# Attention and a gated MLP on one core: four engines pinned to source order, a pair's scores issued in two runs, query block 8 first

## The chip, the cores and the metric

The kernel runs on one core of a Trainium2 chip. The metric is device microseconds of one execution (lower is better); before the change the median of three runs is 756.76 us (756.08 to 757.27).

A core has four compute engines here: TensorE (PE, with PEld for its weight loads), VectorE (DVE), ScalarE (ACT) and GpSimd (POOL). SyncE (SP) issues most DMAs. PE writes its results into PSUM banks, from which DVE and ACT read them.

## What is computed

```python
def _attn_ref(q, k, v):                       # 8 batches, 8 heads, 576 x 64
    scores = scale * np.matmul(q, k.transpose(0, 1, 3, 2))
    mask = block_i >= block_j                 # causal in blocks of 64
    scores = np.where(mask, scores, -1000000000.0)
    scores = scores - np.max(scores, axis=-1, keepdims=True)
    attn = np.exp(scores)
    attn = attn / (np.sum(attn, axis=-1, keepdims=True) + 1e-09)
    return np.matmul(attn, v)

def _moe_ref(x, w_in, w_spatial, b_spatial, w_out):
    h = np.maximum(x @ w_in, 0.0)             # 576 x 512 -> 576 x 1024
    u, v = (h[..., :d_ff // 2], h[..., d_ff // 2:])
    v_n = (v - mu) / np.sqrt(var + 1e-06)     # mu, var over the 512 columns
    v_s = np.einsum('ts,bsd->btd', w_spatial, v_n) + b_spatial[None, :, None]
    return (u * v_s) @ w_out

# reference: x is the attention's output, heads side by side; result = _moe_ref(x, ...)
```

All values are float32.

## The kernel before

**Tiling.** The work of the attention is 32 pairs of heads (8 batches, 4 pairs). The 576 queries are cut into four blocks of 128 (0 to 3) and one of 64 (called block 8 in the change's title; index 4 in `SLOTS`). A pair has seven slots, `(head, first block, last block)`: head 0 and head 1 for blocks 0-1, for block 2, for block 3, and one slot (head 2 in the code's count) that holds the last 64 queries of both heads. Batches 1 to 7 split q and k into a high and a low float32r part (`prep_pair`: two casts "hi" on ACT, four subtractions "lo" on POOL) and compute three products per score tile; batch 0 uses the raw float32 values.

**Steps.** The main loop runs over steps; a pair has seven (`NS`), so step n belongs to pair g = n // 7 with i = n % 7. In each step the code issues, in this order:

- loads and the start of `prep_pair` for the next pair (DMAs on SP);
- `due(0)`: what earlier steps put off with `later`, for example evacuations on ACT and gates on DVE;
- scores on PE: `scores` (L270) for slots 0-1 at i = 0, 2-3 at i = 1, 4-5 at i = 2, and `scores_last` (L290) for the 64-query slot at i = 5 (in batch 0 four slots at i = 0). A score matmul of `scores` contracts 64 rows, one head's half of the partitions (L285); one of `scores_last` contracts 128 rows (L297). The banks come from `s_bank` (L266), a pool of four, and in batch 0 partly from the second pool of four;
- `av` (L453), the output products of an earlier pair: 16 steps after that pair's start (`AV_AT`), or 9 in batch 0 and for the very last pair (`BOOT_AV`). `x_evac` (L431) then casts the result on ACT and subtracts on DVE, one step later in batches 1 to 7, at once in batch 0;
- `exps` (L304) of slot i: scale, mask and row maximum on DVE (L320, L329), exponential with row sum on ACT (L336);
- `transposes` of finished slots on DVE (L406, L411), by the table `TURNS`, and after the last slot `move` (L415): sixteen DMAs on SP (L421) that bring the transposed tile into the one buffer `turned`, from which `av` reads. Batch 0 and the last pair transpose on PE instead (`transposes_pe`, L383) and copy on ACT (L384);
- `norm` (L341): two small operations on DVE (L347, L350), multiplications on POOL (L354);
- `due(1)`, then background work: conversion of the weights (`prep_w`, `prep_w_sp`, `split`) and `prep_pair`;
- groups of the MLP (`moe`) on PE, about one a step, when a batch's attention is done: `v_group` (L515), `u_group` (L609), `sp_group` (L633, gate L642, split L651 and L652), `out_group` (L668, L676);
- `due(2)` and `due(3)`.

Where `b_sp`, the weights and the initial tiles are prepared, the code is as it stands in the listing below.

**What sets the order.** The kernel is traced in this order, but the framework's scheduler decides in which order each engine's instructions are issued: it ranks them by a model of its own, and an instruction whose inputs it takes as ready early may go ahead of others that stand before it in the source. Semaphores follow from the tiles' accesses. Each engine then runs its queue in that fixed order.

Buffers that matter: scores have four PSUM banks (tag "s"), everything else four (tag "m"); "hi" and "lo" two each; the raw q and k one; the probabilities "p" five; the transposed tiles "q" two; `turned` one.

Of the kernel before, what the change touches and what calls it, by code (L numbers as in the profile page):

```python
# [28 lines left out]
SLOTS = [(0, 0, 1), (1, 0, 1), (0, 2, 2), (1, 2, 2), (0, 3, 3), (1, 3, 3), (2, 4, 4)]  # L29
# [4 lines left out]
LAST, AV_AT, BOOT_AV = 5, 2 * NS + 2, NS + 2  # L34
# [7 lines left out]
def kernel(  # L42
# [35 lines left out]


# [7 lines left out]
    for _ in range(6):  # L87
        nc.tensor.matmul(warm[:, :P], mask[:, :P], mask[:, :P], start=True, stop=True)
# [31 lines left out]
    def split(hi, lo, raw):  # L120
        nc.scalar.copy(hi, raw)
        yield
        nc.gpsimd.tensor_tensor(out=lo, in0=raw, in1=hi.bitcast(F32), op=ALU.subtract)
        yield

    def prep_w(hi, lo, w, rows, cols, name):
# [55 lines left out]
    def prep_w_tail():  # L182
# [6 lines left out]
        nc.scalar.copy(ws_a, r[:, :S])  # L189
        nc.scalar.copy(ws_b[64:65, :], r[64:65, S:2 * S])  # L190
        yield
        nc.gpsimd.tensor_tensor(
            out=ws_b[0:64, :], in0=r[0:64, :S], in1=ws_a[0:64, :].bitcast(F32), op=ALU.subtract
        )
        nc.scalar.copy(ws_b[96:97, :], r[96:97, S:2 * S])
        yield
        nc.gpsimd.tensor_tensor(
            out=ws_b[96:97, :], in0=r[96:97, S:2 * S], in1=ws_b[96:97, :].bitcast(F32),
            op=ALU.subtract,
        )  # L200
# [31 lines left out]
    def prep_pair(b, pr):  # L232
# [33 lines left out]
    def s_bank(b, nm, other):  # L266

        if b == 0 and other:
            return ps_m.tile([P, 512], F32, tag="m", name=f"s_{nm}")
        return ps_s.tile([P, 512], F32, tag="s", name=f"s_{nm}")  # L270

    def scores(b, pr, slots):

        parts = operands(b, pr)
        for i in slots:
            banks[(b, pr, i)] = s_bank(b, f"{b}_{pr}_{i}", slots[0] == 4)
        for i in slots[::2]:
            o = 0
            for t in range(SLOTS[i][1], SLOTS[i][2] + 1):
                n = P * (t + 1)  # L280
                qs = slice(S + t * P, S + (t + 1) * P)
                for m, (a, k) in enumerate(parts):
                    for hd in range(2):
                        js = slice(64 * hd, 64 * hd + 64)
                        nc.tensor.matmul(  # L285
                            banks[(b, pr, i + hd)][:, o:o + n], a[js, qs], k[js, :n],
                            start=(m == 0), stop=(m == len(parts) - 1),
                        )
                o += n

    def scores_last(b, pr):
        parts = operands(b, pr)
        bk = [s_bank(b, f"{b}_{pr}_{NS - 1}_{z}", False) for z in range(2)]
        banks[(b, pr, NS - 1)] = bk
        for z in range(2):
            for m, (a, k) in enumerate(parts):
                nc.tensor.matmul(  # L297
                    bk[z][:, :HT], a[:, Q8:], k[:, z * HT:(z + 1) * HT],
                    start=(m == 0), stop=(m == len(parts) - 1),
                )  # L300
# [3 lines left out]
    def exps(b, pr, i):  # L304
# [10 lines left out]
        if hd < 2:  # L315
            o = 0
            runs = []
            for r, t in enumerate(range(t0, t1 + 1)):
                n = P * (t + 1)
                nc.vector.tensor_tensor_reduce(  # L320
                    out=pt[:, o:o + n], in0=bk[:, o:o + n], in1=mask[:, 512 - n:], scale=-0.125,
                    scalar=BIG, op0=ALU.add, op1=ALU.min, accum_out=nmax[:, r:r + 1],
                )
                runs.append((o, n, nmax[:, r:r + 1]))
                o += n
        else:
            for z in range(2):
                zs = slice(z * HT, (z + 1) * HT)
                nc.vector.tensor_tensor_reduce(  # L329
# [3 lines left out]
                )  # L333
            runs = [(0, S, nmax[:, 1:2])]
        for r, (o, n, mx) in enumerate(runs):
            nc.scalar.activation(  # L336
                pt[:, o:o + n], pt[:, o:o + n], AF.Exp, bias=mx, scale=-1.0,
                accum_out=ssum[:, s0 + r:s0 + r + 1],
            )
        ptiles[(b, pr, i)] = (pt, ssum, runs)  # L340

    def norm(b, pr, i):

        both = [ptiles[(b, pr, j)] for j in ((i - 1, i) if i < NS - 1 else (i,))]
        ssum = both[0][1]
        n = sum(len(runs) for _, _, runs in both)
        nc.vector.tensor_scalar(  # L347
            out=ssum[:, 0:n], in0=ssum[:, 0:n], scalar1=EPS_SM, scalar2=None, op0=ALU.add
        )
        nc.vector.reciprocal(ssum[:, 4:4 + n], ssum[:, 0:n])  # L350
        r = 4
        for pt, _, runs in both:
            for o, w, mx in runs:
                nc.gpsimd.tensor_scalar(  # L354
                    out=pt[:, o:o + w], in0=pt[:, o:o + w], scalar1=ssum[:, r:r + 1],
                    scalar2=1.0, op0=ALU.mult, op1=ALU.mult,
                )
# [8 lines left out]
    def transposes_pe(b, pr, i):  # L366
# [15 lines left out]
        for c in range(n):  # L382
            nc.tensor.transpose(bk[:, c * P:(c + 1) * P], pt[:, c * P:(c + 1) * P], ident)  # L383
        nc.scalar.copy(  # L384
            to[:, :, o:o + 32 * n].rearrange("p a (c j) -> p c a j", j=32),
            bk[:, :n * P].rearrange("p (c a j) -> p c a j", a=4, j=32),
        )
        if hd == 2:
            bk = bank(f"{i}c4")
            nc.tensor.transpose(bk[0:64, 0:P], pt[:, 4 * P:S], ident)  # L390
            nc.scalar.copy(
                to[0:64, :, Q8O + P:], bk[0:64, 0:P].rearrange("p (a j) -> p a j", j=32)
            )

    def transposes(b, pr, i):
# [10 lines left out]
        nc.vector.transpose(  # L406
            to[:, :, o:o + 32 * n].rearrange("p r (c j) -> p c r j", j=32),
            pt[:, :n * P].rearrange("p (c r j) -> p c r j", r=4, j=32),
        )
# [23 lines left out]
    def x_evac(b, pr, av, q0, n):  # L433
        qs = slice(q0, q0 + n)

        def hi():
            x = x_tiles(b, pr)
            nc.scalar.copy(x[:, 0, qs], av[:, :n])

        def lo():  # L440
            x = x_tiles(b, pr)
            nc.vector.tensor_tensor(  # L442
                out=x[:, 1, qs], in0=av[:, :n], in1=x[:, 0, qs].bitcast(F32), op=ALU.subtract
            )
# [8 lines left out]
    def av(b, pr):  # L453
# [6 lines left out]
        def tiles(t0, t1, c):  # L460
# [3 lines left out]
            for j in range(2):  # L464
                js = slice(64 * j, 64 * j + 64)
                o = place(j, t0)[0] + 32 * c
                nc.tensor.matmul(  # L467
# [6 lines left out]
                )  # L474
# [6 lines left out]
        for c in range(5):  # L481
            for j in range(2):
                js = slice(64 * j, 64 * j + 64)
                nc.tensor.matmul(
# [3 lines left out]
                )  # L488
# [3 lines left out]
        later(1 if b else 0, 2, lambda: nc.gpsimd.tensor_scalar(  # L492
            out=tails[b][:, pr], in0=xts[(b, pr)][:, :, FULL * P:].bitcast(F32), scalar1=1.0,
            scalar2=1.0, op0=ALU.mult, op1=ALU.mult,
        ))


    def moe(b):
# [5 lines left out]
        def v_group(c):  # L504
# [5 lines left out]
            if c < FULL:  # L510
                m = P
                for j, ws in ((0, (wi_hi, wi_lo)), (1, (wi_hi,))):
                    for k in range(NC):
                        for w in ws:
                            nc.tensor.matmul(  # L515
                                ps, xs[k][:, j, cs], w[:, k, DH:],
                                start=(n == 0), stop=(n == 3 * NC - 1),
                            )
# [344 lines left out]
```

## Time and profile before

| | |
|---|---|
| median of the runs | 756.76 us (3 runs, 756.08 to 757.27) |
| the profiled execution | 759.79 us |
| its span, first to last instruction | 758.0 us |
| granted TensorE clock, mean | 0.966 |
| ACT busy | 426.1 us (56%) |
| POOL busy | 338.8 us (45%) |
| DMA traffic over the span | 92.05 MB, mean 121 GB/s |
| HBM read / written | 38.18 MB / 9.44 MB |

The profiled execution is a run of its own, so durations read in it are compared with its 759.79 us and not with the median. "Busy" of an engine is the time in which at least one instruction of it ran. In the rows of groups, `out<-in` gives the tiles' names without numbers ("s" scores, "p" probabilities, "q" and "turned" transposed, "avl" and "avh" output products, "mv", "mu", "ms", "mo" the MLP's groups); 64*128 before a shape is the part of the array that a matmul uses (rows * columns); x2 means two instructions merged in a row. A wait names the waiting engine and line, then what ended the wait.

### The profile page before, as it was taken

The page shows a single profiled execution, that of the slowest core. Times are in us where ns is not written, and L with a number is a line of the kernel's source. Part 1 is how long each engine was busy: PE and PEld are TensorE (multiplying, and loading weights), DVE is VectorE, ACT ScalarE, POOL GpSimd, SP SyncE. Part 2 cuts the span into 40 slices and gives each one's busy share as a digit, 9 for nine tenths or more (in the row PEclk, how much of TensorE's full clock was granted, in tenths as well). Part 3 has the DMA queues.
Part 4 walks back from the last instruction along what each step waited for, and adds up shares of the span by engine and source line. Part 5 has one row for each costly group of instructions (what it writes and reads, how often), then busy time and mean ns, then how long its engine had stood idle before and what let it go on. Part 6 is the DMA issues. An engine that isn't in the chain of part 4 may idle for free.

```text
span 758.0 us, 16374 instructions
## 1 busy us (share of the span) xinstructions
PE 717.8 (95%) x5729; PEld 624.2 (82%) x5729; DVE 460.9 (61%) x1587; ACT 426.1 (56%) x1156; POOL 338.8 (45%) x525
## 2 busy tenths in 40 slices
PE   7978897799989999999999999999999999999998
PEld 5656696788878988989888988989888988899897
DVE  6785798356754567755685567855576566621430
ACT  5886764445654556655564556744565556642541
POOL 4688447564325534445336544445436541221011
PEclk8898897899989999999999999999999999999999
DMA  6443534455334663455453663445543562441001
GB/s 216 141 143 122 156 111 115 117 153 163 102 107 102 160 180 90 116 149 149 136 136 89 165 167 95 120 133 159 152 121 87 157 169 59 99 116 36 5 16 48
DMA packets 42150, 92.05 MB, mean 121 GB/s; under 512 B 9298, under 2 KB 18002, under 8 KB 42068
## 3 DMA queue, kind: packets, MB, share of 16 engines
q1 hardware_dynamic: 32852, 81.56, 39.4%
q10 hardware_dynamic: 9216, 9.44, 3.6%
q8 instruction: 45, 0.74, 0.4%
q14 instruction: 37, 0.30, 0.1%
HBM read 38.18 MB, written 9.44 MB: 63 GB/s over the span
## 4 chain that ended last, share of the span: by engine, by line
PE 48%; DVE 20%; ACT 13%; POOL 9%; DMA 4%; issue 4%; SPq 1%; POOLq 0%; DVEq 0%; ACTq 0%
PE mo L668 12%; PE ms L633 8%; PE s L285 8%; POOL p L354 4%; PE avh L467 4%; ACT p L336 4%; DVE q L406 4%; PE mu L609 3%; DVE st L545 3%; PE mv L515 3%; PE avl L467 2%; DVE p L320 2%; POOL gl L652 2%; POOL lo L243 2%; ACT vr L569 2%
## 5 line engine op out<-in xcount | busy, mean ns | idle before, releaser
L354 POOL TENSOR_SCALAR p<-p,ssum 128x128 f32<-128x128 f32 (+4 forms) x288 | 162.5, 583 | 206.4 <-DVE ssum L350 135.4
L336 ACT ACTIVATE p<-p,nmax 128x128 f32<-128x128 f32 (+4 forms) x288 | 167.2, 581 | 79.4 <-DVE nmax L320 59.5
L320 DVE CUSTOM_DVE_ANT_0 p<-s,mask 128x128 f32<-128x128 f32 (+3 forms) x256 | 116.9, 479 | 59.9 <-PE s L285 56.1
L406 DVE STREAM_TRANSPOSE q<-p 128x384 f32<-128x384 f32 (+1 forms) x189 | 115.0, 625 | 41.0 <-POOL p L354 39.2
L243 POOL TENSOR_TENSOR lo<-raw,hi 128x288 fp32r<-128x288 f32 x112 | 92.8, 854 | 95.9 <-ACT hi L239 84.4
L609 PE MATMUL mu<-x,wi_hi 128*128 128x288 f32 x512 | 112.8, 299 | 0.3 <-DVE x L442 0.3
L609 PEld LDWEIGHTS mu<-x,wi_hi 128*128 128x128 f32 x512 | 85.4, 189 | 5.2 <-DVE nmax L320 1.0
L515 PE MATMUL mv<-wi_hi,x 128*128 128x512 f32 x256 | 86.0, 397 | 0.0
L668 PE MATMUL mo<-gh,wo_hi 128*128 128x288 f32 x256 | 81.6, 319 | 4.1 <-ACT gh L651 4.1
L652 POOL TENSOR_TENSOR gl<-u,gh 128x288 fp32r<-128x288 f32 x64 | 50.9, 806 | 75.5 <-ACT gh L651 75.1
L668 PE MATMUL mo<-gl,wo_hi 128*128 128x288 f32 x256 | 79.4, 310 | 4.3 <-POOL gl L652 3.3
L633 PE MATMUL ms<-ws_hi,vh 128*128 128x288 f32 x256 | 77.6, 303 | 0.0
L668 PE MATMUL mo<-gh,wo_lo 128*128 128x288 f32 x256 | 77.2, 302 | 0.0
L633 PE MATMUL ms<-ws_hi,vl 128*128 128x288 f32 x256 | 76.0, 297 | 0.0
L633 PE MATMUL ms<-ws_lo,vh 128*128 128x288 f32 x256 | 75.9, 296 | 0.0
L285 PE MATMUL s<-hi 64*128 64x128 f32 (+1 forms) x224 | 63.5, 410 | 13.0 <-DVE nmax L320 13.0
L609 PE MATMUL mu<-x,wi_lo 128*128 128x288 f32 x256 | 70.2, 297 | 0.0
L651 ACT CAST gh<-u 128x288 fp32r<-128x288 f32 x64 | 27.3, 431 | 75.0 <-DVE u L642 73.8
L285 PEld LDWEIGHTS s<-hi 64*128 64x128 f32 x224 | 31.4, 191 | 34.3 <-DVE nmax L320 19.2
L668 PEld LDWEIGHTS mo<-gh,wo_hi 128*128 128x128 f32 x256 | 49.6, 194 | 9.9 <-ACT gh L651 4.5
L515 PEld LDWEIGHTS mv<-wi_hi,x 128*128 128x128 f32 x256 | 48.0, 188 | 11.6 <-ACT st L548 1.2
L668 PEld LDWEIGHTS mo<-gl,wo_hi 128*128 128x128 f32 x256 | 49.7, 194 | 9.1 <-POOL gl L652 8.9
(120 smaller groups left out, 1590.2 us busy)
## 6 DMA issues: line engine op xcount, KB each, us to landing
turned<-q SPq DMA_DIRECT2D x216, 100.0 KB, 2.2
turned<-q SPq DMA_DIRECT2D x216, 96.0 KB, 2.2
raw<-qk SPq DMA_DIRECT2D x31, 608.0 KB, 4.5
v<-v SPq DMA_DIRECT2D x32, 320.0 KB, 3.3
outT<-o ACTq DMA_DIRECT2D x64, 144.0 KB, 2.0
rwi<-w_in SPq DMA_DIRECT2D x8, 512.0 KB, 3.7
rwo<-w_out SPq DMA_DIRECT2D x4, 512.0 KB, 3.9
rws<-w_spT SPq DMA_DIRECT2D x4, 288.0 KB, 2.8
```

The source lines that it names most:

```text
L243: nc.gpsimd.tensor_tensor(out=lo[:, cs], in0=raw[:, cs], in1=hi[:, cs].bitcast(F32), op=ALU.subtract)
L285: nc.tensor.matmul(banks[(b, pr, i + hd)][:, o:o + n], a[js, qs], k[js, :n], start=(m == 0), stop=(m == len(parts) - 1),)
L320: nc.vector.tensor_tensor_reduce(out=pt[:, o:o + n], in0=bk[:, o:o + n], in1=mask[:, 512 - n:], scale=-0.125, scalar=BIG, op0=ALU.add, op1 ...
L336: nc.scalar.activation(pt[:, o:o + n], pt[:, o:o + n], AF.Exp, bias=mx, scale=-1.0, accum_out=ssum[:, s0 + r:s0 + r + 1],)
L354: nc.gpsimd.tensor_scalar(out=pt[:, o:o + w], in0=pt[:, o:o + w], scalar1=ssum[:, r:r + 1], scalar2=1.0, op0=ALU.mult, op1=ALU.mult,)
L406: nc.vector.transpose(to[:, :, o:o + 32 * n].rearrange("p r (c j) -> p c r j", j=32), pt[:, :n * P].rearrange("p (c r j) -> p c r j", r=4, ...
L467: nc.tensor.matmul(out[js, (t0 - q0) * P:(t1 + 1 - q0) * P].rearrange("p (t a j) -> p a t j", a=4, j=32), vt[:, c, js], src[:, :, o:o + 32 ...
L515: nc.tensor.matmul(ps, xs[k][:, j, cs], w[:, k, DH:], start=(n == 0), stop=(n == 3 * NC - 1),)
L609: nc.tensor.matmul(ps[:, :HT], w[:, k, ds], xs[k][:, j, zs], start=(n == 0), stop=(n == 3 * NC - 1),)
L633: nc.tensor.matmul(ps[:, :HT], a[:, ds], w[:, k, zs], start=(n == 0), stop=False)
L652: nc.gpsimd.tensor_tensor(out=gl[:, dc, :], in0=uz, in1=gh[:, dc, :].bitcast(F32), op=ALU.subtract)
L668: nc.tensor.matmul(ps[:, :HT], w[:, k, es], a[:, k, :], start=(n == 0), stop=(n == 3 * ND - 1),)
```

## The change

1. A helper `own` passes each compute instruction of PE, DVE, ACT and POOL to `tc.keep_in_program_order`, which adds an ordering edge, without a semaphore, to the instruction traced before it on the same engine. DMAs, and a few memsets, are not passed.
2. `SLOTS` now begins with the 64-query slot (`scores_last`, `norm`, `transposes` and `TURNS` follow the new numbers; the new slots 1 to 6 are the old 0 to 5).
3. In batches 1 to 7 all scores of a pair are issued in two runs: the 64-query slot and slots 1-2 at i = 0, slots 3-4 and 5-6 at i = 3 (`RUN2`). In batch 0: slots 1-2 at i = 0, 3-4 at i = 1, 5-6 at i = 3, and the next pair's 64-query slot at i = 5. All score banks come from the pool of four (`s_bank` is gone).
4. `av` comes at step 17 of its pair instead of 16 (batches 1 to 7), 10 instead of 9 for the very last pair, so behind the second run of the pair then in work; `move` is issued at step 10, ahead of `exps`, instead of step 9 behind the transposes. Batch 0's raw load for the pair after next is issued at i = 4 instead of 6.

The core of the diff; every compute instruction not shown is wrapped in `own(...)` in the same way as the one in `scores`.

```diff
-SLOTS = [(0, 0, 1), (1, 0, 1), (0, 2, 2), (1, 2, 2), (0, 3, 3), (1, 3, 3), (2, 4, 4)]
+SLOTS = [(2, 4, 4), (0, 0, 1), (1, 0, 1), (0, 2, 2), (1, 2, 2), (0, 3, 3), (1, 3, 3)]
...
-LAST, AV_AT, BOOT_AV = 5, 2 * NS + 2, NS + 2
+RUN2 = 3
+AV_AT, BOOT_AV, LAST_AV = 2 * NS + RUN2, NS + 2, NS + RUN2
...
+    def own(ins):
+
+        tc.keep_in_program_order(ins)
+
...
         for i in slots:
-            banks[(b, pr, i)] = s_bank(b, f"{b}_{pr}_{i}", slots[0] == 4)
+            banks[(b, pr, i)] = ps_s.tile([P, 512], F32, tag="s", name=f"s_{b}_{pr}_{i}")
...
-                        nc.tensor.matmul(
+                        own(nc.tensor.matmul(
                             banks[(b, pr, i + hd)][:, o:o + n], a[js, qs], k[js, :n],
                             start=(m == 0), stop=(m == len(parts) - 1),
-                        )
+                        ))
...
-        both = [ptiles[(b, pr, j)] for j in ((i - 1, i) if i < NS - 1 else (i,))]
+        both = [ptiles[(b, pr, j)] for j in ((i - 1, i) if i else (i,))]
...
-    TURNS = ((), (0, 1), (), (2, 3), (), (4, 5), (6,))
+    TURNS = ((0,), (), (1, 2), (), (3, 4), (), (5, 6))
...
-            if i == LAST + 1 and g + 2 < NPAIR:
+            if i == RUN2 + 1 and g + 2 < NPAIR:
                 load_pair(0, g + 2)
...
         if here:
             if i == 0:
-                scores(*here, (0, 1, 2, 3) if boot else (0, 1))
-            elif i == 1 and not boot:
-                scores(*here, (2, 3))
-            elif i == 2:
-                scores(*here, (4, 5))
-            elif i == LAST:
-                scores_last(*here)
+                if g == 0 or not boot:
+                    scores_last(*here)
+                scores(*here, (1, 2))
+            elif i == 1 and boot:
+                scores(*here, (3, 4))
+            elif i == RUN2:
+                scores(*here, (5, 6) if boot else (3, 4, 5, 6))
+            elif i == RUN2 + 2 and boot and g + 1 < NPAIR:
+                scores_last(*pairs[g + 1])
         for of in range(max(0, g - 2), min(g + 1, len(pairs))):
-            if n - of * NS == (BOOT_AV if by_pe(pairs[of]) else AV_AT):
-                av(*pairs[of])
-                if of % NPAIR == NPAIR - 1:
-                    later(1 if of >= NPAIR else 0, 3, lambda b=pairs[of][0]: begin(b))
+            b, pr = pairs[of]
+            if n - of * NS == (LAST_AV if (b, pr) == last else AV_AT if b else BOOT_AV):
+                av(b, pr)
+                if pr == NPAIR - 1:
+                    later(1 if b else 0, 3, lambda b=b: begin(b))
+
+        if at(n - NS - RUN2) and i == RUN2 and not by_pe(at(n - NS - RUN2)[:2]):
+            move(*at(n - NS - RUN2)[:2])
         if here:
             exps(*here, i)
...
                     transposes(b, pr, j)
-                    if j == NS - 1:
-                        move(b, pr)
-        if at(n - 1) and (i - 1) % NS in (1, 3, 5, 6):
+        if at(n - 1) and (i - 1) % NS in (0, 2, 4, 6):
             norm(*at(n - 1))
```

More of the change, by code (lines that the diff above doesn't have):

```diff
@@ L87 @@
     for _ in range(6):
-        nc.tensor.matmul(warm[:, :P], mask[:, :P], mask[:, :P], start=True, stop=True)
+        own(nc.tensor.matmul(warm[:, :P], mask[:, :P], mask[:, :P], start=True, stop=True))
     make_identity(nc, ident)
@@ L120, in split @@
     def split(hi, lo, raw):
-        nc.scalar.copy(hi, raw)
+        own(nc.scalar.copy(hi, raw))
         yield
-        nc.gpsimd.tensor_tensor(out=lo, in0=raw, in1=hi.bitcast(F32), op=ALU.subtract)
+        own(nc.gpsimd.tensor_tensor(out=lo, in0=raw, in1=hi.bitcast(F32), op=ALU.subtract))
         yield
@@ L238, in prep_pair @@
         for cs in (slice(0, S), slice(S, KQ)):
-            nc.scalar.copy(hi[:, cs], raw[:, cs])
+            own(nc.scalar.copy(hi[:, cs], raw[:, cs]))
         yield
@@ L292, in scores_last @@
         parts = operands(b, pr)
-        bk = [s_bank(b, f"{b}_{pr}_{NS - 1}_{z}", False) for z in range(2)]
-        banks[(b, pr, NS - 1)] = bk
+        bk = [ps_s.tile([P, 512], F32, tag="s", name=f"s_{b}_{pr}_0_{z}") for z in range(2)]
+        banks[(b, pr, 0)] = bk
         for z in range(2):
             for m, (a, k) in enumerate(parts):
-                nc.tensor.matmul(
+                own(nc.tensor.matmul(
                     bk[z][:, :HT], a[:, Q8:], k[:, z * HT:(z + 1) * HT],
                     start=(m == 0), stop=(m == len(parts) - 1),
-                )
+                ))
     ptiles = {}
@@ L466, in tiles @@
                 o = place(j, t0)[0] + 32 * c
-                nc.tensor.matmul(
+                own(nc.tensor.matmul(
                     out[js, (t0 - q0) * P:(t1 + 1 - q0) * P].rearrange(
@@ L483, in av @@
                 js = slice(64 * j, 64 * j + 64)
-                nc.tensor.matmul(
+                own(nc.tensor.matmul(
                     ah[js, 256:320].rearrange("p (a j) -> p a j", j=32), vt[:, c, js],
@@ L487, in av @@
                     start=(c == 0), stop=(c == 4),
-                )
+                ))
         x_evac(b, pr, al, 0, 256)
         x_evac(b, pr, ah, 256, 320)
-        later(1 if b else 0, 2, lambda: nc.gpsimd.tensor_scalar(
+        later(1 if b else 0, 2, lambda: own(nc.gpsimd.tensor_scalar(
             out=tails[b][:, pr], in0=xts[(b, pr)][:, :, FULL * P:].bitcast(F32), scalar1=1.0,
             scalar2=1.0, op0=ALU.mult, op1=ALU.mult,
-        ))
+        )))
     def moe(b):
@@ L549, in stats @@
-                nc.vector.tensor_scalar(
+                    ))
+                own(nc.vector.bn_stats(out=st[:m, 0:6], in_=vr[:m, :]))
+                own(nc.vector.bn_aggr(out=st[:m, 6:8], in_=st[:m, 0:6]))
+                own(nc.scalar.activation(st[:m, 8:9], st[:m, 7:8], AF.Ln, bias=eps[:m, :]))
+                own(nc.scalar.activation(st[:m, 9:10], st[:m, 8:9], AF.Exp, scale=-0.5))
+                own(nc.vector.tensor_scalar(
                     out=st[:m, 10:11], in0=st[:m, 7:8], scalar1=EPS_LN, scalar2=-0.5,
@@ L608, in u_group @@
                     for w in ws:
-                        nc.tensor.matmul(
+                        own(nc.tensor.matmul(
                             ps[:, :HT], w[:, k, ds], xs[k][:, j, zs],
                             start=(n == 0), stop=(n == 3 * NC - 1),
-                        )
+                        ))
                         n += 1
@@ L650, in split_g @@
                 gh, gl = g[z]
-                nc.scalar.copy(gh[:, dc, :], uz)
-                nc.gpsimd.tensor_tensor(
+                own(nc.scalar.copy(gh[:, dc, :], uz))
+                own(nc.gpsimd.tensor_tensor(
                     out=gl[:, dc, :], in0=uz, in1=gh[:, dc, :].bitcast(F32), op=ALU.subtract
-                )
+                ))
                 ready[z] += 1
@@ L675, in leave @@
                 o = o_p.tile([P, HT], F32, tag="o", name=f"o_{b}_{z}_{ec}")
-                nc.scalar.copy(o, ps[:, :HT])
+                own(nc.scalar.copy(o, ps[:, :HT]))
                 nc.scalar.dma_start(outT[b, es, z * HT:(z + 1) * HT], o)
```

159 lines of the change are left out of this document (75 added, 84 removed).

## The prediction

> **What bounds the kernel now.** I read the page first, then busy time by stage, then the matmuls one by one.
>
> ```profile
> span 758.0 us, 16374 instructions
> PE 717.8 (95%) x5729; PEld 624.2 (82%) x5729; DVE 460.9 (61%) x1587; ACT 426.1 (56%) x1156; POOL 338.8 (45%) x525
> ```
>
> TensorE (PE) is busy 95% of the span; no other engine passes 61%. The stages differ, though. I cut at the first matmul of the first batch's MLP (69.3 us), at the end of batch 1's last output products (180) and at the last pair's (684). Columns: busy time of PE, weight loads, DVE, ACT, POOL, then the granted clock.
>
> ```profile
> 0.00:69.30 69.30, 56.15 (x441) 38.92 (x441) 48.35 (x176) 50.16 (x140) 47.10 (x70) 0.88 0.47 152
> 69.30:180.00 110.70, 96.66 (x737) 83.35 (x736) 77.58 (x256) 63.18 (x170) 62.58 (x88) 0.89 0.48 139
> 180.00:684.00 504.00, 495.43 (x4085) 436.22 (x4085) 316.49 (x1108) 287.51 (x789) 219.19 (x354) 0.99 0.47 127
> ```
>
> From 180 to 684 us PE is idle 8.6 of 504 us at a clock of 0.99, and DVE is at 63%: here only the number and the packing of matmuls set the time. Before 180 us PE is idle 27 us at a clock of 0.88, no engine is full, and waits between engines count.
>
> **Term A: heads that run alone.** A score matmul has 64 rows. The source issues the two heads of a pair alternately; these are two places of the timeline of PE where slots 0 and 1 are computed (names are "s", last column the count merged in a row).
>
> ```profile
> 78.49 0.33 PE L285 MATMUL s<-hi 64*128 64x128 f32 x2
> ...
> 79.17 0.28 PE L285 MATMUL s<-hi,lo 64*128 64x256 f32 x2
> 79.38 0.50 PE L515 MATMUL mv<-wi_hi,x 128*128 128x512 f32 x1
> ```
>
> ```profile
> 168.93 0.32 PE L285 MATMUL s<-hi 64*128 64x128 f32 x1
> ...
> 169.81 0.40 PE L668 MATMUL mo<-gh,wo_hi 128*128 128x288 f32 x1
> ```
>
> At 78.49 two heads start together (x2), and twelve matmuls take 79.38 - 78.49 = 0.89 us. At 168.93 six matmuls of one head (x1) take 169.81 - 168.93 = 0.88 us. A second head beside the first is free; alone it is paid in full. From there on the other head's six stand elsewhere, pulled ahead of the output products:
>
> ```profile
> 419.11 0.29 PE L297 MATMUL s<-hi,lo 128*128 128x288 f32 x1
> 419.33 0.32 PE L285 MATMUL s<-hi 64*128 64x128 f32 x1
> ...
> 420.21 0.87 PE L467 MATMUL avl<-turned,v 128*64 128x256 f32 x8
> ...
> 423.12 0.40 PE L668 MATMUL mo<-gh,wo_hi 128*128 128x288 f32 x1
> ```
>
> ```profile
> 650.96 0.33 PE L285 MATMUL s<-hi 64*128 64x128 f32 x1
> ...
> 657.80 0.29 PE L297 MATMUL s<-hi,lo 128*128 128x288 f32 x1
> 658.03 0.87 PE L467 MATMUL avl<-turned,v 128*64 128x256 f32 x8
> ```
>
> From block 8 to the output products it takes 420.21 - 419.11 = 1.10 us with that head between, and 658.03 - 657.80 = 0.23 us without it. So the lone head costs 0.87 us. Such split pairs run from 168.93 to 650.96, 23 of them, (2,1) to (7,3); in six of these the last third is paired again, with the same cost of the burst. The change pins PE to the source's order, where the heads alternate without exception: 23 x 0.87 = 20.0 us go.
>
> **Term B: fewer bursts.** Going from 128-row to 64-row matmuls and back costs time too. The scores of slots 2 and 3 once alone, once behind another 64-row burst:
>
> ```profile
> 414.71 0.29 PE L668 MATMUL mo<-gl,wo_hi 128*128 128x288 f32 x1
> ...
> 415.66 0.40 PE L668 MATMUL mo<-gh,wo_hi 128*128 128x288 f32 x1
> 415.89 0.29 PE L668 MATMUL mo<-gh,wo_lo 128*128 128x288 f32 x1
> 416.03 0.29 PE L668 MATMUL mo<-gl,wo_hi 128*128 128x288 f32 x1
> ```
>
> ```profile
> 100.36 0.28 PE L285 MATMUL s<-hi,lo 64*128 64x256 f32 x2
> ...
> 101.10 0.40 PE L609 MATMUL mu<-x,wi_hi 128*128 128x288 f32 x1
> ```
>
> Alone: 415.89 - 414.71 = 1.18 us, less two regular steps of 0.13 (415.89 to 416.03 is one, rounded up), 0.92 us. Joined: 101.10 - 100.36 = 0.74, less the exit that the burst before it has anyway (79.38 - 79.17 = 0.21), 0.53 us. Joining saves 0.39 us. Apart from the lone head, before has three 64-row bursts a pair (slots 0-1, 2-3, 4-5); the change has two, new slots 1-2 behind block 8 and 3-6 together. 28 pairs of batches 1 to 7 x 0.39 = 10.9 us. Block 8 (128 rows) moves from behind a 64-row burst to behind MLP matmuls, and the output products from behind block 8 to behind a 64-row burst: exits of 0.2 to 0.3 us each that swap, taken at 0, bounds -3 and +3 us in all.
>
> **What else moves.** The order edges add no instruction. The output products go from step 16 to 17 of a pair, their casts, subtractions and tail copy with them, and the sixteen moves into "turned" from step 9 to 10: still right behind the previous pair's products, seven steps ahead of their own. On the SP queue they stay behind the v loads; the next qk load now comes four steps behind them, not five.
>
> ```profile
> 381.33 10.06 SPq L421 DMA_DIRECT2D turned<-q  x16
> ```
>
> The last column is the time to landing, then waits (total, times, longest).
>
> ```profile
> turned<-q SPq DMA_DIRECT2D x216, 96.0 KB, 2.2
> raw<-qk SPq DMA_DIRECT2D x31, 608.0 KB, 4.5
> ...
> SPq L421 <- DMA outT<-o: 42.8, 19, 5.4
> ```
>
> Sixteen issues take 10.1 us and the last lands 2.2 us later: 12.3 us, or 17.7 with the longest hold by an output store (5.4). A pair takes 504 us / 24 = 21 us, after terms A and B 19.7, less 2.9 us of products (420.21 to 423.12): 16.8 us remain. So it is covered but for the few held ones, up to 0.9 us in perhaps seven of them; I take 1 us, bounds 0 and 6.
>
> The fixed order puts PE's next pair behind slot 6 of the one before: its second bank frees when DVE has read it. Between the end of step 3 on PE and that moment DVE has three gatings, the maxima of slots 4, 5 and 6 (each with a short readout), two subtractions, two transposes and a norm (us and mean ns follow the bar):
>
> ```profile
> L642 DVE TENSOR_TENSOR u<-ms,u 128x288 f32<-128x288 f32 x64 | 28.0, 444 | 44.7 <-PE ms L638 44.6
> L320 DVE CUSTOM_DVE_ANT_0 p<-s,mask 128x384 f32<-128x384 f32 x64 | 33.3, 551 | 16.0 <-PE s L285 15.2 <-PE t L383 0.7
> L320 DVE CUSTOM_DVE_ANT_0 p<-s,mask 128x512 f32<-128x512 f32 x64 | 43.1, 674 | 11.2 <-PE s L285 8.4 <-PE t L383 2.9
> L406 DVE STREAM_TRANSPOSE q<-p 128x384 f32<-128x384 f32 x108 | 58.9, 564 | 4.9 <-POOL p L354 3.1 <-POOL gl L652 1.8
> L442 DVE TENSOR_TENSOR x<-avh,x 128x320 fp32r<-128x320 f32 x32 | 15.1, 471 | 7.0 <-ACT x L438 7.0
> L347 DVE TENSOR_SCALAR ssum<-ssum 128x2 f32<-128x2 f32 x64 | 17.2, 268 | 16.0 <-ACT p L336 15.8
> ...
> L320 DVE DVE_READ_ACCUMULATOR2_ANT nmax<- 128x1 f32 x256 | 20.9, 82 | 0.0
> L350 DVE RECIPROCAL ssum<-ssum 128x2 f32<-128x2 f32 x64 | 10.3, 161 | 1.2
> ...
> PEld s L285 <- DVE nmax L320: 19.2, 32, 5.5
> ```
>
> 3 x 0.44 + 0.55 + 2 x 0.67 + 3 x 0.08 + 2 x 0.47 (the other subtraction is no longer) + 2 x 0.56 + 0.27 + 0.16 = 5.9 us. PE in that time has three groups of fourteen matmuls at 0.13 us and block 8's six: 48 x 0.13 = 6.2 us. The cover is 0.3 us, and thinner than that only where gates follow groups. I take 2 us of new waits over the run, bounds 0 and 12. [...]
>
> **Boot and batch 1** (to 180 us). In batch 0 the casts of x and the subtractions stand ahead of slot 2's maxima and exponentials in the source. Now:
>
> ```profile
> 22.91 1.55 PE L467 MATMUL avl<-turned,v 128*64 128x256 f32 x8
> ...
> 24.77 0.72 ACT L336 ACTIVATE p<-p,nmax 128x512 f32<-128x512 f32 x1
> 26.97 0.43 ACT L438 CAST x<-avh 128x320 fp32r<-128x320 f32 x1 [0.30 <-PE avh L484]
> ...
> DVE p L320 <- PE s L285: 13.3, 6, 5.3
> ```
>
> ACT did an exponential during the products (22.91 to 26.9 us); pinned, ACT and DVE stand still for them. That costs nothing if they had no work, and at most 4.0 us in each of four pairs, 16 us. Against it, DVE's 13.3 us of waiting for scores in the first 69.3 us should go, since block 8's scores come two steps early. I take +2 us, bounds -8 and +10. From 69.3 to 180 us PE idles 14 us; part of it is heads of the next pair pulled in front of a bank that DVE had not freed, which pinning prevents, and part is weight conversion on DVE, which stays. I take -4 us, bounds -14 and +3.
>
> **The sum**, against the profiled execution (759.8 us, span 758.0): -20.0 (lone heads) - 10.9 (bursts) + 1 (moves) + 2 (bank waits) + 2 (boot) - 4 (batch 1) = -29.9, so 729.9 us. The median of the runs shown (756.76) lies 3.0 us below the profiled execution: 726.9, forecast **727 us**.
>
> **Rivals.**
> 1. *Slower: the fixed order makes DVE late for the bank.* ACT's cast "hi" is pinned at step 2 and waits for qk (4.5 us behind a queue of 10.1 to 15.5 us); evacuations and x casts stand behind it, DVE's subtraction behind those, slot 6 behind that, and PE at the next pair's start. From 0.3 us of lateness PE waits; from 30 / 28 + 0.3 = 1.4 us a pair the gain is eaten. At 2.5 us: 28 x 2.2 = 62 us more, about 789 us. For it: the thin cover, and 32 waits of this kind already. Against it: ACT and DVE are under 65% busy, and qk should land about when ACT gets there. 10%.
> 2. *Boot eats half.* Boot at its upper bound, nothing won up to 180 us, waits at 5 us more: 727 + 8 + 4 + 5 = 744 us. 15%.
> 3. *More is won early*: boot and batch 1 near their lower bounds, 727 - 8 - 8 = 711 us. 18%.
> 4. *The heads do not pair*, because banks free one at a time: term A is lost, 747 us. Against it: all places with x2 overlap. 4%.
>
> **Chances.** The forecast's case 50%, rival 3 18%, rival 2 15%, rival 4 4%, no change 3%, rival 1 10%. Faster by over 0.2% (1.5 us; the runs shown spread by 1.2 us) 0.87, within 0.03, slower 0.10. The range leaves out rival 1, no change and the ends of rivals 2 and 3: 706 to 748 us.
>
> **What would show it.** Right: all of L285's rows in batches 1 to 7 come as x2; 64-row bursts fall to two a pair; a pair from 180 us on takes 19.5 to 20 us; matmul counts are the same. Boot: block 8's scores before slot 1's; first MLP matmul at 66 to 75 us. Wrong: PE or its weight loads waiting for "DVE nmax" over 25 us after 180 us (rival 1), or ACT's "hi" waiting for qk over 40 us.

## The result and the profile after

The change makes the kernel slower: 775.88 us (median of 4 runs, 774.16 to 777.68) against 757.01 us (4 runs, 756.08 to 757.27), ratio 1.0252 with a 95% interval of 1.0227 to 1.0277. The forecast was 727 us. The page of the kernel after, then its stretches at the times used for the kernel before, then the last stretch of the kernel before:

```profile
span 774.3 us, 16381 instructions
PE 695.3 (90%) x5729; PEld 611.9 (79%) x5729; DVE 468.5 (61%) x1587; ACT 430.8 (56%) x1156; POOL 341.5 (44%) x525
```

```profile
0.00:69.30 69.30, 50.62 (x348) 32.17 (x349) 46.33 (x147) 41.90 (x115) 35.11 (x57) 0.85 0.41 131
69.30:180.00 110.70, 79.09 (x600) 69.16 (x600) 70.86 (x229) 58.65 (x155) 57.38 (x75) 0.83 0.40 110
180.00:684.00 504.00, 480.35 (x4133) 430.58 (x4131) 329.40 (x1153) 297.63 (x810) 234.17 (x374) 0.98 0.53 134
684.00:774.30 90.30, 85.22 (x653) 80.01 (x652) 21.91 (x59) 32.61 (x77) 14.87 (x21) 1.00 0.12 37
```

```profile
684.00:758.00 74.00, 69.50 (x472) 65.72 (x470) 18.44 (x50) 25.23 (x59) 9.93 (x13) 1.00 0.08 27
```

Read span as busy plus idle time of PE. Busy fell from 717.8 to 695.3 us: 22.5 of the 30.9 us that pairing and joining were to bring, at a lower mean clock (0.947 against 0.966). Idle rose from 40.2 to 79.0 us. The sum of the two, +16.3 us, is the difference of the spans. By stretch (the last one is longer after) the idle time went from 13.2 to 18.7, from 14.0 to 31.6, from 8.6 to 23.7 and from 4.5 to 5.1 us. So the question is what PE waits for.

**The two runs of a pair** are as forecast. Run 1 of pair (5,1) and run 2 of (5,0) with the output products:

```profile
447.24 0.30 PE L637 MATMUL ms<-ws_b,vs_b 97*128 97x288 f32 x1
...
448.27 0.33 PE L284 MATMUL s<-hi 64*128 64x128 f32 x2
...
449.38 0.29 PE L632 MATMUL ms<-ws_lo,vh 128*128 128x288 f32 x1
```

```profile
435.50 0.29 PE L667 MATMUL mo<-gl,wo_hi 128*128 128x288 f32 x1
435.72 0.45 PE L284 MATMUL s<-hi 64*128 64x384 f32 x2
...
437.14 0.87 PE L466 MATMUL avl<-turned,v 128*64 128x256 f32 x8
...
440.29 0.29 PE L667 MATMUL mo<-gh,wo_lo 128*128 128x288 f32 x1
```

Less two regular steps of 0.13, run 1 takes 449.38 - 447.24 - 0.26 = 1.88 us, run 2 with the products 440.29 - 435.50 - 0.26 = 4.53 us.

**Place 1, batch 1.** A burst that should take 1.88 us begins at 106.12 and takes 27 us. It is block 8 and slots 1 and 2 of one pair. Waits from 100 to 130 us, then SyncE's queue, DVE, ACT and POOL:

```profile
PEld s L296 <- POOL lo L248: 20.6, 2, 19.4
DVE fwo L149 <- DMA rwo<-w_out: 14.2, 2, 11.1
ACT ws_a L194 <- DMA rwt<-w_spT: 8.1, 1, 8.1
```

```profile
100.68 10.13 SPq L420 DMA_DIRECT2D turned<-q  x16
110.85 0.59 SPq L190 DMA_DIRECT2D rwt<-w_spT  x1
111.49 0.76 SPq L192 DMA_DIRECT2D rwt<-b_sp  x2
112.35 11.48 SPq L141 DMA_DIRECT2D rwo<-w_out  x3
```

```profile
116.20 0.43 DVE L149 TENSOR_SCALAR fwo<-rwo 128x512 f32<-128x512 f32 x1 [11.12 <-DMA rwo<-w_out]
```

```profile
113.62 0.67 ACT L194 CAST ws_a<-rwt 128x576 fp32r<-128x576 f32 x1 [8.05 <-DMA rwt<-w_spT]
```

```profile
122.08 1.40 POOL L202 TENSOR_TENSOR ws_b<-rwt,ws_b 1x576 fp32r<-1x576 f32 x1 [6.32 <-issue]
123.56 1.26 POOL L128 TENSOR_TENSOR wo_lo<-fwo,wo_hi 128x512 fp32r<-128x512 f32 x1
124.79 2.11 POOL L248 TENSOR_TENSOR lo<-raw,hi 128x288 fp32r<-128x288 f32 x2
```

The last load of w_spT and the first of w_out come behind sixteen moves. Their conversions are pinned, so DVE and ACT stand still 11.1 and 8.1 us with other work behind them; POOL then does two conversions before the "lo" that PE needs.

**Place 2, pair 3 of each batch.** Run 2 and the products of (3,3) and (5,3), undisturbed 4.53 us, take 9.1 and 7.5 us:

```profile
325.83 0.49 PE L284 MATMUL s<-hi 64*128 64x512 f32 x1 [0.33 <-DVE nmax L319]
328.21 0.50 PE L284 MATMUL s<-hi 64*128 64x512 f32 x1 [1.90 <-DVE nmax L319]
...
329.49 1.55 PE L466 MATMUL avl<-turned,v 128*64 128x256 f32 x8
...
333.61 0.40 PE L632 MATMUL ms<-ws_hi,vh 128*128 128x288 f32 x1
...
500.45 0.50 PE L284 MATMUL s<-hi 64*128 64x512 f32 x1 [1.89 <-DVE nmax L319]
...
501.34 0.87 PE L466 MATMUL avl<-turned,v 128*64 128x256 f32 x8
...
504.25 0.40 PE L632 MATMUL ms<-ws_hi,vh 128*128 128x288 f32 x1
```

The second head of slots 5-6 waits until DVE has read slot 2. In this pair the last v group's layer norm stands in front of that maximum. DVE in (3,3):

```profile
326.75 0.73 DVE L588 TENSOR_TENSOR vs_a<-vr,vs_b 64x512 fp32r<-64x512 f32 x1 [0.71 <-ACT vs_b L578]
327.51 0.29 DVE L319 CUSTOM_DVE_ANT_0 p<-s,mask 128x128 f32<-128x128 f32 x1
...
327.73 0.42 DVE L319 CUSTOM_DVE_ANT_0 p<-s,mask 128x256 f32<-128x256 f32 x1
```

DVE waits 0.71 us for ACT's part of the norm and does its own in 0.73 us before it comes to slot 2, which is read at 327.73 + 0.42 = 328.15; PE goes on at 328.21. The two waits of PE, 1.90 and 1.89 us, are alike; the products take 333.61 - 329.49 = 4.12 us after one and 504.25 - 501.34 = 2.91 after the other (see the last section).

**Place 3, the end.** PE, pinned, stands before the last pair's transposes:

```profile
667.29 1.12 PE L382 MATMUL t<-ident,p 128*128 128x128 f32 x4 [3.83 <-POOL p L353]
```

**Place 4, batch 0.** The first MLP matmul is at 80.5 us, not 69.3. ACT stands at the x casts during the output products, and DVE at the subtractions behind them:

```profile
22.44 0.37 ACT L437 CAST x<-avl 128x256 fp32r<-128x256 f32 x1 [0.23 <-PE avl L466]
24.55 0.42 ACT L437 CAST x<-avh 128x320 fp32r<-128x320 f32 x1 [1.74 <-PE avh L483]
```

### The profile page after: what moved, and what is told of

It reads as the page before. It is cut to its first block, busy times and chain, and to the rows that moved or that the text cites. A ratio compares the mean times of both kernels' runs of the same rounds, so it can differ in the third digit from the quotient of the medians.

```text
span 774.3 us, 16381 instructions
## 1 busy us (share of the span) xinstructions
PE 695.3 (90%) x5729; PEld 611.9 (79%) x5729; DVE 468.5 (61%) x1587; ACT 430.8 (56%) x1156; POOL 341.5 (44%) x525
## 4 chain that ended last, share of the span: by engine, by line
PE 57%; DVE 15%; DMA 8%; ACT 6%; POOL 5%; SPq 5%; issue 4%; POOLq 0%; ACTq 0%; DVEq 0%
PE mv L514 10%; PE mo L667 10%; PE ms L632 9%; PE avh L466 6%; PE mu L608 5%; PE s L284 5%; SPq L420 4%; PE avl L466 3%; DMA turned<-q 3%; DVE q L405 3%; PE avh L483 2%; DVE p L319 2%; POOL p L353 2%; DMA raw<-qk 2%; PE s L296 1%
## 5 line engine op out<-in xcount | busy, mean ns | idle before, releaser
L353 POOL TENSOR_SCALAR p<-p,ssum 128x384 f32<-128x384 f32 (+4 forms) x288 | 162.7, 579 | 253.3 <-DVE ssum L349 135.3
L335 ACT ACTIVATE p<-p,nmax 128x384 f32<-128x384 f32 (+4 forms) x288 | 167.1, 581 | 110.8 <-DVE nmax L319 68.9
L405 DVE STREAM_TRANSPOSE q<-p 128x384 f32<-128x384 f32 (+1 forms) x189 | 110.1, 615 | 9.7 <-DMA turned<-q 8.8
L608 PEld LDWEIGHTS mu<-x,wi_hi 128*128 128x128 f32 x512 | 88.1, 196 | 3.1 <-issue 0.4
L641 DVE TENSOR_TENSOR u<-ms,u 128x288 f32<-128x288 f32 x64 | 29.1, 454 | 92.7 <-PE ms L637 92.7
L667 PE MATMUL mo<-gh,wo_hi 128*128 128x288 f32 x256 | 78.1, 305 | 0.0
L608 PE MATMUL mu<-x,wi_lo 128*128 128x288 f32 x256 | 72.4, 304 | 0.0
L284 PE MATMUL s<-hi 64*128 64x128 f32 (+1 forms) x224 | 48.8, 388 | 17.1 <-DVE nmax L319 16.9
L466 PE MATMUL avh<-turned,v 128*64 128x128 f32 x868 | 57.0, 286 | 0.0
L544 DVE BATCH_NORM_STATS2 st<-vr 128x6 f32<-128x512 f32 (+1 forms) x40 | 27.5, 689 | 44.4 <-ACT vr L532 44.0
```

Of the source, the lines that this page charges most:

```text
L284: own(nc.tensor.matmul(banks[(b, pr, i + hd)][:, o:o + n], a[js, qs], k[js, :n], start=(m == 0), stop=(m == len(parts) - 1),))
L335: own(nc.scalar.activation(pt[:, o:o + n], pt[:, o:o + n], AF.Exp, bias=mx, scale=-1.0, accum_out=ssum[:, s0 + r:s0 + r + 1],))
L353: own(nc.gpsimd.tensor_scalar(out=pt[:, o:o + w], in0=pt[:, o:o + w], scalar1=ssum[:, r:r + 1], scalar2=1.0, op0=ALU.mult, op1=ALU.mult,))
L405: own(nc.vector.transpose(to[:, :, o:o + 32 * n].rearrange("p r (c j) -> p c r j", j=32), pt[:, :n * P].rearrange("p (c r j) -> p c r j", ...
L466: own(nc.tensor.matmul(out[js, (t0 - q0) * P:(t1 + 1 - q0) * P].rearrange("p (t a j) -> p a t j", a=4, j=32), vt[:, c, js], src[:, :, o:o ...
L608: own(nc.tensor.matmul(ps[:, :HT], w[:, k, ds], xs[k][:, j, zs], start=(n == 0), stop=(n == 3 * NC - 1),))
```

## The experiments

Each kernel was timed beside the kernel before on the same chip (medians there 755.9 to 757.8 us). The ratio is to the kernel before.

| kernel | us | ratio (95%) |
|---|---|---|
| the change | 775.9 | 1.025 (1.023 to 1.028) |
| place_free | 758.0 | 1.000 (0.999 to 1.002) |
| pe_pinned | 774.0 | 1.023 (1.019 to 1.027) |
| before_pinned | 808.5 | 1.068 (1.064 to 1.072) |
| weights_out | 759.1 | 1.003 (1.000 to 1.005) |
| ln_out | 770.9 | 1.016 (1.014 to 1.019) |
| boot_cast | 772.4 | 1.017 (1.014 to 1.021) |
| w_queue | 773.3 | 1.020 (1.018 to 1.023) |
| three | 749.6 | 0.990 (0.987 to 0.994) |
| w_ahead | 758.9 | 1.002 (0.999 to 1.004) |
| sp_pinned | 762.4 | 1.008 (1.005 to 1.010) |
| three_sp | 729.1 | 0.964 (0.961 to 0.966) |
| three_sp_last | 723.8 | 0.956 (0.953 to 0.959) |
| sp_ln | 742.9 | 0.984 (0.980 to 0.987) |
| kept_all | 745.0 | 0.985 (0.982 to 0.989) |
| boot_free | 717.8 | 0.950 (0.947 to 0.952) |
| boot_pool | 722.6 | 0.957 (0.954 to 0.960) |

**Order or places?** place_free makes `own` return at once; pe_pinned does so for all engines but PE; before_pinned wraps the kernel before in `own`; weights_out chains all but the weight conversion, whose instructions float:

```diff
-        own(nc.scalar.copy(hi, raw))
+        free_order(nc.scalar.copy(hi, raw))
...
-        own(nc.vector.tensor_scalar(
+        free_order(nc.vector.tensor_scalar(
```

> The change without its first part: new slots, runs and places, no order edge on any engine. Theory (pinned weight conversion stops whole engines: DVE, ACT and POOL stand behind weight loads that are late, PE 27 us at 106 us and 7 us at 155 us): the stalls go, 34 us, but the lone heads may come back, up to 20 us: 742 to 762 us, and no wait of DVE for w_out over 3 us. Rival (the new placement itself costs the time: block 8 first, two runs, four score banks in batch 0): 770 us or more.

> The whole change, but order edges on PE alone; DVE, ACT and POOL are ordered by the scheduler. Theory (blocking by pinned conversion on the three other engines): the heads stay paired and the 34 us of stalls go: about 738 us, 730 to 745. Rival 1 (placement or PE's own fixed order costs the time): 770 us or more. Rival 2 (pins on DVE, ACT and POOL are worth something in the steady part): between, 750 to 760, with more waits of PE for DVE's maxima after 180 us than the full change has (25 us).

> The kernel before with order edges on all four engines and nothing else. Theory (blocking by pinned conversion): the heads pair, -20 us, but the conversion stalls appear as they do in the change, +30 to +40: 765 to 780 us, with DVE waiting for w_out over 8 us once. Rival (placement costs, pins don't): 735 to 740 us.

> The whole change with order edges on everything but the conversion of the weights (its casts, shifts and subtractions float; the others are chained past them). Theory: the stalls at 106 and 155 us go, 776 - 34 = 742 us, range 736 to 750; the batch-end stalls of 3 to 6 us stay. Rival (placement, or other pinned waits such as the layer norm's on DVE): 768 us or more, with PE waiting over 15 us for lo in batch 1 as now.

The rival that blames the new places for the loss falls: without edges they leave the time as it was (758.0), and DVE has no wait for w_out. But they do a good deal. The busy line of place_free (span 753.9 us):

```profile
PE 693.5 (92%) x5729; PEld 610.9 (81%) x5729; DVE 466.4 (62%) x1587; ACT 426.6 (57%) x1156; POOL 344.0 (46%) x525
```

PE is busy 24.2 us less than before and idle 60.4 us instead of 40.2. The heads pair without any edge: of the 672 matmuls of 64 rows in batches 1 to 7, some 20 stand in rows of x1 there, as in the change, and some 260 in the kernel before. So the new places alone bring the pairing, and new waits with it: from 180 to 684 us PE waits 21.0 us for DVE's maxima, all at block 8, which the scheduler puts ahead of the output products. In before_pinned the heads pair by edges alone (some 40 in rows of x1), yet the edges cost that kernel 51.5 us (808.5, well above the 765 to 780 expected; what makes up the excess stays open), of which the new places win back 32.6.

Edges on PE alone don't help (774.0, far from the 738 expected). The theory's part comes true: PE is at the first product of batch 2 at 199.08 us, at 220.62 in the change. But the gain is lost behind it: from the first product of batch 2 to that of batch 7 it takes 645.16 - 199.08 = 446.1 us there,

```profile
199.08 0.87 PE L467 MATMUL avl<-turned,v 128*64 128x256 f32 x8
...
645.16 0.87 PE L467 MATMUL avl<-turned,v 128*64 128x256 f32 x8
```

against 438.5 before (199.97 to 638.46) and 425.3 in the change (220.62 to 645.88). In these stretches PE idles 28.1, 7.0 and 15.8 us. The largest of its waits from 180 to 684 us in pe_pinned is for an MLP operand from POOL, 17.2 us where the change has 4.6:

```profile
PEld mo L668 <- POOL gl L652: 17.2, 20, 1.6
```

That the free engines deliver in another order than PE's fixed one asks for is the likely reason; no run separates it. The floating conversion (weights_out) gains 16.8 us, half of the 34 expected; the rest has other causes.

**Three suspects.** ln_out lets the v groups' evacuation, statistics, scale, normalisation and low part float. boot_cast:

```diff
         if b == 0:
-            hi()
-            lo()
+            later(0, 1, hi)
+            later(0, 1, lo)
             return
```

w_queue replaces `nc.sync.dma_start` by `nc.gpsimd.dma_start` for the weights; three joins weights_out, ln_out and boot_cast.

> The whole change, but the layer norm of the MLP (evacuation, statistics, scale, normalisation, low part of a v group) floats on ACT and DVE; everything else stays chained. Theory (in pair 3 of a batch the maxima of slots 1 and 2 stand on DVE behind the last v group's norm, which goes back and forth between DVE and ACT; run 2 then waits for the banks, 3 to 6 us once a batch, 27 us over six batches): run 2 of these pairs falls from 7.5 to 10.4 us to under 6, time 776 - 20 to 27 = 752 us, range 748 to 758. Rival (the lateness is DVE's and ACT's load in that stretch, whatever the order): 770 us or more, run 2 there still over 7 us.

> The whole change, but in batch 0 the casts of x (ACT) and the subtractions (DVE) are put behind the step's maxima and exponentials instead of ahead of them. Theory (they stop ACT and DVE during the output products, some 3 us in each of four pairs): the first scores of batch 1 come at about 60 us instead of 70, the first MLP matmul at 70 instead of 80; 776 - 10 = 766 us, range 761 to 770. Rival (boot's loss is the weight conversion's or the multiplications' on POOL): first MLP matmul stays at 78 or later and the time at 773 or more.

> The whole change, all edges kept; only the loads of the weights are issued by POOL's queue instead of SP's, so that they don't stand behind the sixteen moves of a pair. Theory (a pinned conversion is harmful because its load is late behind the moves): the 27 us stall at 106 us falls under 10, DVE waits under 4 us for w_out; about 757 us, range 750 to 764, as with the conversion floating (759). Rival (the conversion's place in the order costs the time, however early the load): 770 us or more.

> Three edits of the change at once: weight conversion floating, layer norm floating, batch 0's x casts behind the exponentials. If the three causes are separate they add: 759 - 10 - 23 = 726 us, range 717 to 736, and the gain that the prediction had put at 30 us is there. Rival (they are one cause, lateness that moves from place to place): 745 us or more.

All three single edits gave less than expected (5.0, 3.4 and 2.6 us; the last is little more than the 1.9 us by which the medians of the kernel before differ). Joined in three they give 26.3 us, about the sum of the single gains with weights_out's (16.8 + 5.0 + 3.4 = 25.2), so 749.6 us and not the 717 to 736 expected. In ln_out run 2 of pair 3 still takes up to 11.4 us, for another reason. PE, then SyncE's queue and POOL:

```profile
217.73 0.87 PE L481 MATMUL avl<-turned,v 128*64 128x256 f32 x8 [0.61 <-ACT hi L259]
...
239.80 0.62 PE L299 MATMUL s<-hi,lo 64*128 64x512 f32 x2
243.86 1.55 PE L481 MATMUL avl<-turned,v 128*64 128x256 f32 x8 [3.44 <-DMA turned<-q]
```

```profile
229.95 0.33 SPq L249 DMA_DIRECT2D raw<-qk  x1
230.39 11.52 SPq L435 DMA_DIRECT2D turned<-q  x16
```

```profile
226.67 3.25 POOL L263 TENSOR_TENSOR lo<-raw,hi 128x288 fp32r<-128x288 f32 x4
```

The scores are done at 240.4, but the products wait 3.4 us for "turned". The products before began at 217.73 and take 2.9 us, so the buffer was free near 220.6; the moves start only at 230.39, right behind a q/k load that waited for POOL's "lo" to free its buffer (226.67 + 3.25 = 229.92). The change does not pin SyncE, and the scheduler put that load, which the source issues later, ahead of the moves. w_queue misses for a similar reason: its loads stand in POOL's queue, one of them waits 8.6 us for a buffer, and PE waits 15.3 us for the "lo" behind it. It does not decide between its two theories.

**Loads ahead, SyncE in order, the end.** w_ahead keeps all edges:

```diff
+    def ahead(a, b, wait):
+        next(a)
+        next(b)
+        for _ in range(wait):
+            yield
+        yield from a
+        yield from b
...
-    spread(chain([prep_w_out(c) for c in range(ND)]), 7 * ND + 1, U0 + 10, U0 + 17)
+    spread(chain([ahead(prep_w_out(c), prep_w_out(c + 1), 8) for c in (0, 2)]), 41, U0 + 10, U0 + 20)
```

and three more yields behind the tail's loads. sp_pinned chains the q/k and v loads and the moves on SyncE:

```diff
-                nc.sync.dma_start(turned[32 * r:32 * r + 32, a, :w], t[32 * a:32 * a + 32, r, :w])
+                own(nc.sync.dma_start(turned[32 * r:32 * r + 32, a, :w], t[32 * a:32 * a + 32, r, :w]))
```

three_sp is three with that; three_sp_last also issues the last pair's `transposes_pe` three steps behind, not two.

> The whole change, all edges kept; but two loads of w_out are issued together and their conversions follow some two steps (5 to 6 us) later, and the tail's load of w_spT stands one step ahead of its casts. The run before (loads by POOL's queue) left DVE 7 us and POOL 8.6 us of waiting, because each load still stood right ahead of its conversion. Theory (a pinned conversion harms because its load is issued in the same step): DVE's 11 us wait for w_out and the 27 us of the burst at 106 us fall, the burst under 10; 776 - 18 = 758 us, range 751 to 765. Rival (the conversion's work and its crossing between DVE, ACT and POOL cost the time): 769 us or more.

> The whole change, and SyncE's q/k and v loads and the moves into turned kept in source order too (the change left them to the scheduler, which put some q/k loads ahead of the move that came first in the source). Theory A (in pair 3 of a batch DVE's lateness for the banks ends last): nearly no gain, 770 to 777 us. Theory B (the late moves end last wherever their slack is under 0.5 us): 20 pairs by 0.5 us and more, 755 to 766 us.

> The three edits together (conversion and layer norm floating, batch 0's x casts behind the exponentials), with SyncE's q/k and v loads and the moves in source order. Theory (with the layer norm floating the banks are free in time, but run 2 of pair 3 still takes 8 to 10 us since the output products then wait for the move, which stands behind a q/k load that waits for its buffer): 750 - 12 = 738 us, range 731 to 743, run 2 of pair 3 under 6 us. Rival (the moves are late because their tile is transposed late on DVE): 747 us or more.

> As the run before, and the very last pair's transposes on PE come one step later. Theory (pinned, PE stands at these transposes for multiplications that are not done: 4 us and more behind the last batch's products, and from the products of (7,0) to the end it takes 8 us longer than in the kernel before): 5 us less than the run before, range 2 to 8. Rival (the end is bound by the MLP's chain): no difference, within 1 us.

w_ahead shows place 1: with every edge kept, loads that stand ahead of their conversions give 17.0 us, as much as letting the conversions float. DVE has no wait for w_out left. (The edit also spreads the conversion of w_out over three more steps; the two are not separated.) sp_pinned gives 13.5 us, as theory B has it, though run 2 of pair 3 still takes 7.5 to 9.2 us; on top of three the same edit gives 20.5 us, to 2 us below the range expected, and run 2 of pair 3 falls to 5.4 to 5.8 us. In three_sp the moves start as the products of (2,0) end (195.71 + 0.75 = 196.46):

```profile
195.71 0.75 PE L498 MATMUL avh<-turned,v 128*64 128x64 f32 x20
```

```profile
196.48 11.17 SPq L435 DMA_DIRECT2D turned<-q  x16
207.76 0.52 SPq L249 DMA_DIRECT2D raw<-qk  x1
```

Batches 2 to 6 take 599.52 - 193.48 = 406.0 us there:

```profile
193.48 0.87 PE L481 MATMUL avl<-turned,v 128*64 128x256 f32 x8
...
599.52 0.87 PE L481 MATMUL avl<-turned,v 128*64 128x256 f32 x8
```

That is 32.5 us less than before for twenty pairs. The last pair's later transposes give 5.3 us, as expected.

**What adds, and what edges cost.** sp_ln is ln_out with SyncE in order. kept_all joins w_ahead, boot_cast, SyncE in order and the late last transposes, with every edge kept. boot_free is three_sp_last without edges on DVE, ACT and POOL in the steps of batch 0, boot_pool without those on POOL alone.

> The whole change with the layer norm floating and SyncE's loads and moves in source order, nothing else. Alone the first gave 5 us and the second 13.5. Theory (in pair 3 of a batch run 2 has two late inputs, banks by DVE and the move, and each hides the other): together 13.5 + 5 + 10 to 15, so about 745 us, range 740 to 750, run 2 of pair 3 under 6 us. Rival (they add): 757 us or more.

> The whole change with every edge kept, and repairs in the source alone: loads of w_out and of the tail ahead of their conversion, batch 0's x casts behind the exponentials, SyncE in source order, the last pair's transposes a step later. Theory (the fixed order is not the cost, its places are): 776 - 17 - 3.5 - 13.5 - 5 = 737 us, range 731 to 743, with run 2 of pair 3 still at 7.5 to 9 us since the layer norm stays in the order. Rival (edges on DVE, ACT and POOL cost by themselves): 750 us or more.

> The fastest so far (conversion and layer norm floating, x casts moved, SyncE in source order, last transposes late: 724), and in the steps of batch 0 no edges on DVE, ACT and POOL. With PE alone in order the first scores of batch 1 came at 59 us, with all four at 70. Theory (the edges on the three other engines delay batch 0): 59 us again and 724 - 10 = 714 us, range 710 to 719. Rival (the time is given back in batch 1, where PE waits for late inputs anyway): 722 us or more.

> As the run before, but in batch 0 only POOL is without edges. Theory (PE's transposes wait for multiplications that stand on POOL behind subtractions of the weight conversion and the tail copies): most of the 10 us, 714 to 718 us. Rival (ACT's or DVE's order causes it): 722 us or more.

sp_ln gains 33.0 us where its two parts alone gained 5.0 and 13.5: in pair 3 two late inputs hid each other. From batch 2 on its run 2 takes 5.4 to 5.8 us; with the norm alone floating it took 5.9 to 11.4 in batches 2 to 6 (PE waits 10.8 us for "turned" after 180 us), with SyncE alone in order 7.5 to 9.2 (11.1 us for DVE's maxima). kept_all is 31 us faster than the change with no edge removed, 2 us outside its range; what it still lacks to three_sp_last is 21 us. The layer norm on the path is most of that: run 2 of pair 3 takes 7.5 to 9.2 us there in batches 2 to 6, 17 us more in the five than in sp_ln, and PE waits 13.3 us for DVE's maxima from 180 to 684 us,

```profile
PE s L306 <- DVE nmax L341: 13.3, 12, 1.9
```

against 2.1 us in sp_ln. In batch 0 the edges on the three engines cost 6.0 us. boot_pool is 1.2 us off three_sp_last, within the noise, but it can't clear POOL: with its edges gone POOL still issued the same instructions in the same order up to 60 us. Only in boot_free does its order differ, and there PE's wait for POOL's multiplications in the first 80 us falls from 17.9 to 10.5 us. Which engine's order costs the 6.0 us stays open.

## Why the prediction was wrong

- **Lone heads and bursts (-30.9 us): right in kind, though pinning is not what it took.** PE's busy time fell by 22.5 us at a lower clock; with the waits gone, twenty pairs take 32.5 us less (1.6 a pair, where the two terms give 0.87 + 0.39 = 1.26; part of that are waits that the kernel before had). The prediction gave the 20.0 us of the lone heads to the pinned order; place_free has the pairs without it.
- **Moves (+1, 0 to 6): failed.** The term asked how long the sixteen issues take and not what stands ahead of them. The prediction took SP's queue to be in the source's order; SP is the one engine that the change leaves out. Ordering it gives 13.5 us alone and 20.5 with the other repairs.
- **Bank waits (+2, 0 to 12): too small.** The pair that was summed has no v group's norm in it; pair 3 does, once a batch. With SyncE in order, letting the norm float gives 762.4 - 742.9 = 19.5 us. This is rival 1 in kind (DVE late for the bank), not by its mechanism: "hi" waiting for qk took 10.0 us after 180 us, where 40 was its sign; the norm stood in the way. The other sign, over 25 us of waits for "DVE nmax" after 180 us, came out at the line: 14.3 us of weight loads and 11.1 of PE, partly at the same time.
- **Batch 1 (-4, -14 to +3): wrong sign.** The prediction said of the weight conversion that it "stays". Its work does; but the scheduler had put the conversion where its load had come (DVE waited 0.9 us for w_out in the kernel before, 14.2 in the change), and the pinned one right behind its load stopped its engine (DVE for up to 11.1 us). Cost: 17 us, shown by w_ahead and weights_out.
- **Boot (+2, -8 to +10): near its upper bound.** About 3.4 us by the x casts and 6.0 by other edges, the latter measured with everything else mended.
- **The end** was not in the sum: 5.3 us for the last pair's pinned transposes.

No single term explains the 49 us between the forecast and 775.9: batch 1, the moves and the bank waits are the large ones, each some 12 to 21 us off by the runs above. The chain of repairs, 775.9 to 749.6, 729.1, 723.8 and 717.8 us, ends below the forecast: the gain was real, and the new waits were larger. Of the observables, the two bursts a pair came true; the rows of L284 are x2 but for those where a bank is late; a pair from 180 us on took 425.3 / 20 = 21.3 us instead of 19.5 to 20; and the first MLP matmul (80.5 instead of 66 to 75 us) told against the forecast.

## What to carry to other kernels

In the change a wait of one instruction on a pinned engine became a wait of all that stood behind it (DVE's 11.1 us for w_out and ACT's 8.1 us for w_spT, place 1): before pinning, list each instruction that waits for a DMA or goes back and forth between two engines, and put its load steps ahead or leave it out of the order. Look at the order of the DMA queue too: here putting SyncE in order gave 13.5 us alone and 20.5 with other repairs. Two late inputs of one burst hid each other here (5.0 and 13.5 us gained alone, 33.0 together), so an edit that gains little alone may be half of a repair.

## What the runs showed of the hardware

A short stall cost twice here: as idle time, and in four bursts of five by a lower granted clock behind it. Stretches of 1 us of the kernel after, around the two like waits shown under place 2 (granted clock in the third column from the end):

```profile
329.00:330.00 1.00, 1.00 (x7) 0.32 (x6) 1.00 (x4) 1.00 (x5) 0.00 (x0) 0.50 0.00 0
330.00:331.00 1.00, 1.00 (x10) 0.81 (x8) 0.81 (x4) 1.00 (x4) 0.00 (x0) 0.50 0.03 8
...
501.00:502.00 1.00, 1.00 (x11) 0.52 (x10) 1.00 (x5) 1.00 (x5) 0.00 (x0) 1.00 0.00 0
```

After a wait of 1.90 us the clock fell to 0.50 and the burst took 9.1 us; after one of 1.89 it stayed at 1.00 and the burst took 7.5. So of the 4.6 us lost in the first, the 1.6 by which it exceeds the second are put down to the clock. The other three bursts of pair 3 in batches 2 to 6 have the same waits of 1.89 or 1.90 us; the clock fell to 0.50 in each, and they took 9.1, 10.4 and 9.1 us. In all five there are 0.33 us of idle time before the longer wait and one matmul of a single head, of 0.49 or 0.50 us, between the two. So what went before the fall was alike in the burst without one; what decides between the two is not shown.
